# Routed experts behind gated linear attention: a tile's rows scaled on ScalarE, summed and written during the next tile

## The chip, the cores and the metric

The kernel runs on one core of a Trainium2 chip. The metric is device time in microseconds, the median of three runs. Before the change these were 812.84, 816.72 and 817.99 us, so the median is 816.72 us.

## The reference

Two blocks follow each other. The first is a gated linear recurrence per batch element and head; the second sends each row of its output to the two best of eight experts (noisy top-2 router) and adds the two weighted answers. All arrays are float32.

```
# attention: B, H, S, D = 4, 8, 768, 48
for t in range(S):
    state = alpha[:, :, t, :, None] * state + einsum('bhd,bhe->bhde', k[:, :, t], v[:, :, t])
    y[:, :, t] = einsum('bhd,bhde->bhe', q[:, :, t], state)
x = y.transpose(0, 2, 1, 3).reshape(3072, 384)

# router and experts: E = 8, F = 1024
noisy = x @ w_gate + log1p(exp(x @ w_noise)) * noise
top2 = the two largest of noisy per row;  w = softmax over these two
out[row] = sum over its two experts e of w_e * (relu(x[row] @ w1[e]) @ w2[e])
```

Each of the 3072 rows is answered by two experts, so every row of `out` is the sum of two weighted terms.

## The kernel before

**The recurrence** goes by 24 chunks of 128 time steps. `fast_gla` gives small functions (`load`, `load_v`, `alphas`, `keys`, `queries`, `scores`, `state`, `output`, ...) that the main loop at the end calls in a written-out order, several chunks deep. `load(n)` brings alpha, k and q of chunk n through the SP queue (L163), `load_v(n)` its v (L167). v of chunk 0 is first read by the matmuls of `state(0)` (L354).

**Routing.** After every three chunks the two experts of each row are found, and an entry (row, weight, expert, rank) is written to a table in DRAM that is sorted by expert (L138). `plan_tiles` then cuts the table into tiles of 128 entries of one expert. These tiles, not the rows in their first order, are the units of the expert work. With this data 51 tiles run.

**A tile i of the experts** is a chain over all engines. Its functions, with the engines they run on:

- `load_tab` (SP, L740): the 128 entries of the tile; `gather_x` (VectorE L757 to L763, then GpSimd L765): which rows these are, and an indirect DMA that gathers the rows of x; `load_w1` (SP, L748): the 1.5 MB of the expert's first matrix, in two buffers.
- `turn_x` (TensorE L774, VectorE L776): x transposed into `xt`, of which there is one buffer.
- `layer1` in two parts (TensorE L785, ScalarE L787): 48 matmuls of 128 columns, ReLU out of PSUM into `h`.
- `layer2` in two parts (TensorE L797): 16 matmuls of 384 columns into `o_ps`. The pool of `o_ps` has one buffer, so the first matmul of the next tile's `layer2` waits until `o_ps` has been read.
- `get_first` (GpSimd L804): an indirect DMA that reads, for entries that are their row's second answer, what the first answer left in `out`, into `prev` (two buffers). It waits for every earlier write to `out`, so for that of the tile before too.
- `combine` (GpSimd L814, VectorE L815, GpSimd L816): `prev` times 0 or 1 (no first answer, or one), then `o_ps` times the weight plus `prev`, then an indirect DMA that writes the rows to `out`.

`tile_steps` groups these into four steps per tile; engines work through their instructions in the order in which the code issues them. Tiles 0 to 9 are issued in between the last pieces of the recurrence and the routing (the main loop hands out the steps of two tiles per round from round 23 on), all later ones alone. The helper `few` borrows a buffer of `h_ps` for small router results (L620, L621, L665, read on VectorE by L622 and L667).

```
        def third():
            if i + 1 < units[1]:
                turn_x(i + 1)
            get_first(i)
            layer2(i, 0)

        def fourth():
            layer2(i, 1)
            combine(i)
```

So GpSimd's order in a steady tile is: gather for tile i + 2, read of the first answers, their scaling, write of the result.

Of the kernel before, what the change touches and what calls it, by code (L numbers as in the profile page):

```python
# [9 lines left out]
F32 = mybir.dt.float32  # L10
U32 = mybir.dt.uint32
I32 = mybir.dt.int32
AF = mybir.ActivationFunctionType
ALU = mybir.AluOpType
# [4 lines left out]
def kernel(  # L19
# [29 lines left out]
    nc = tc.nc  # L49
    B, H, S, D = q.shape  # L50
    N, DM = out.shape
    E, _, F = moe_w1.shape
    C = 128
# [8 lines left out]
    NU = NT // UC  # L62
# [6 lines left out]
    NTILE = (2 * N) // C + E - 1  # L69
    ALWAYS = (2 * N) // C + (E - 1) // 2  # L70
# [6 lines left out]
    def pool(name, bufs, on=ctx, **kw):  # L77
        return on.enter_context(tc.tile_pool(name=name, bufs=bufs, **kw))
# [557 lines left out]
    def put_some(n):  # L636
        for place, entry in to_put[:n]:
            put_entries(place, entry)
        del to_put[:n]
# [83 lines left out]
    def experts(on):  # L723
        one, two, three = on["one"], on["two"], on["three"]
        NB = 3
        x_in = [one.tile([C, DM], F32, name=f"x_in{i}") for i in range(NB)]
        prev = [one.tile([C, DM], F32, name=f"prev{i}") for i in range(2)]
# [1 line left out]
            nc.gpsimd.memset(t, 0.0)  # L729
        WHY = "computed from the counts, in range by construction"  # L730
        tabs, w1s, xts, os_, wheres = {}, {}, {}, {}, {}
        puts, gets = [], []

        def load_tab(i, units):
            if i >= NTILE:
# [67 lines left out]
        def get_first(i):  # L803
# [4 lines left out]
                tc.add_manual_dep(get.ins, put.name, AFTER, reason="reads rows of any earlier tile")  # L808
            gets.append(get.ins)

        def combine(i):
            o_ps, tab, where = os_.pop(i)["ps"], tabs.pop(i), wheres.pop(i)
            rows = prev[i % 2]
            nc.gpsimd.tensor_scalar(out=rows, in0=rows, scalar1=tab[:, 6:7], scalar2=None, op0=ALU.mult)  # L814
            nc.vector.scalar_tensor_tensor(rows, o_ps, tab[:, 1:2], rows, op0=ALU.mult, op1=ALU.add)  # L815
            put = nc.gpsimd.indirect_dma_start(out=out, out_offset=bass.IndirectOffsetOnAxis(ap=where[:, 0:1], axis=0),  # L816
                                               in_=rows, in_offset=None, bounds_check=N - 1, oob_is_err=False)
            for earlier in puts + gets:
                tc.declare_no_dep(put.ins, earlier, reason="different rows, or one that this tile has read")
            puts.append(put.ins)  # L820

        return load_tab, load_w1, gather_x, turn_x, layer1, layer2, get_first, combine


    def tile_steps(i, do, units):
        load_tab, load_w1, gather_x, turn_x, layer1, layer2, get_first, combine = do

        def first():
            if i + 1 < units[1]:
                load_w1(i + 1)  # L830
            if i + 2 < units[1]:
                gather_x(i + 2, units[0])
            layer1(i, 0)

        def second():
            layer1(i, 1)

        def third():
            if i + 1 < units[1]:
                turn_x(i + 1)  # L840
            get_first(i)
            layer2(i, 0)

        def fourth():
            layer2(i, 1)
            combine(i)

        return [first, second, third, fourth]

# [8 lines left out]
    def last_tiles(i, do):  # L858
        if i == NTILE:
            return  # L860
        number = nc.values_load(tiles_i[0:1, 0:1], min_val=0, max_val=NTILE,
                                skip_runtime_bounds_check_because="a count of tiles")
        with tc.If(number > i):
            do[0](i, NU)
            do[1](i)
            do[2](i, NU)
            do[3](i)
            for step in tile_steps(i, do, (NU, i + 1)):
                step()
            last_tiles(i + 1, do)  # L870


    def again_by_levels():
        with ExitStack() as es:
            on = pool("g_clear", 1, es)
            clear_table(on)
        with ExitStack() as es:
            general_gla(es)
        with ExitStack() as es:
            do = experts(pools(es, "g_"))  # L880
            for i in range(4):
                do[0](i, NU)
            do[1](0)
            for i in range(2):
                do[2](i, NU)
            do[3](0)
            for i in range(NTILE):
                do[0](i + 4, NU)
                for step in tile_steps(i, do, (NU, NTILE)):
                    step()  # L890


    with ExitStack() as es:
# [3 lines left out]
        do = experts(on)  # L897
        load_tab, load_w1, gather_x, turn_x = do[:4]
# [4 lines left out]
        def steps_of(i, n):  # L903
            units = NU if n >= NT + 4 else unit_of[i] + 1
            limit = min(ALWAYS, GIVEN[units - 1])
            steps = tile_steps(i, do, (units, limit))
            if i + 4 < limit:
                steps[0] = lambda go=steps[0]: (load_tab(i + 4, unit_of[i + 4] + 1), go())
            return steps
# [7 lines left out]

        with tc.manual_schedule():
            load(0)
            load(1)  # L920
            load_v(0)
            for n in range(2):
                alphas(n)
                keys(n)
# [6 lines left out]
            for n, tiles in enumerate(beside):  # L931
# [8 lines left out]
                last = [lambda: give(n - 3), lambda: put_some(UC)]  # L940
# [66 lines left out]
```

## Time and profile before

| what | value |
|---|---|
| median of three runs | 816.72 us (812.84 to 817.99) |
| the profiled execution | 817.13 us |
| its span, first to last instruction | 815.4 us |
| TensorE busy over the span | 758.8 us (93%) |
| GpSimd / VectorE / ScalarE busy | 347.4 us (43%) / 261.5 us (32%) / 168.8 us (21%) |
| mean granted TensorE clock, as a share of full speed | 0.974 |

The profiled execution is 0.4 us above the median and its span 1.7 us shorter than its own time; what lies outside the span belongs to start and end of the program. A share of busy time is a mean over stages: the first 210 us are recurrence and routing, from then to 800 us expert tiles follow each other. In the rows, PE is TensorE, PEld its weight loads, DVE VectorE, ACT ScalarE, POOL GpSimd, SP the queue that issues most DMAs. The time in square brackets is what the engine sat idle just before, and behind the arrow stands what ended that. A buffer that VectorE releases may be named by an instruction of VectorE just behind the one that did it.

### The profile page before, as it was taken

The page shows a single profiled execution, that of the slowest core. Times are in us where ns is not written, and L with a number is a line of the kernel's source. Part 1 is how long each engine was busy: PE and PEld are TensorE (multiplying, and loading weights), DVE is VectorE, ACT ScalarE, POOL GpSimd, SP SyncE. Part 2 cuts the span into 40 slices and gives each one's busy share as a digit, 9 for nine tenths or more (in the row PEclk, how much of TensorE's full clock was granted, in tenths as well). Part 3 has the DMA queues.
Part 4 walks back from the last instruction along what each step waited for, and adds up shares of the span by engine and source line. Part 5 has one row for each costly group of instructions (what it writes and reads, how often), then busy time and mean ns, then how long its engine had stood idle before and what let it go on. Part 6 is the DMA issues. An engine that isn't in the chain of part 4 may idle for free. (4 is left out here: it accounts for less than half of the span.)

```text
span 815.4 us, 14294 instructions
## 1 busy us (share of the span) xinstructions
PE 758.8 (93%) x5239; PEld 622.7 (76%) x5239; DVE 261.5 (32%) x858; ACT 168.8 (21%) x332; POOL 347.4 (43%) x439
## 2 busy tenths in 40 slices
PE   5999999998999898999999999999999999999992
PEld 4888888887888586877787867787777778777781
DVE  6778877898310224101111011110111111111100
ACT  2465535644111110100111001110011110101100
POOL 4326754656342544434343334433343433433331
PEclk9999979999899999999999999999999999999997
DMA  9999888986645444455445654455554455555420
GB/s 154 173 214 178 201 186 180 186 178 189 229 121 181 150 164 148 159 186 201 165 166 193 210 187 153 167 184 196 182 193 154 157 191 205 208 196 204 161 95 12
DMA packets 152160, 141.76 MB, mean 174 GB/s; under 512 B 114861, under 2 KB 126735, under 8 KB 152084
## 3 DMA queue, kind: packets, MB, share of 16 engines
q1 hardware_dynamic: 139744, 116.51, 51.1%
q0 software_dynamic: 11328, 23.72, 8.1%
q8 instruction: 45, 0.74, 0.4%
q10 hardware_dynamic: 1012, 0.53, 0.3%
q14 instruction: 31, 0.25, 0.1%
HBM read 131.95 MB, written 15.25 MB: 181 GB/s over the span
## 5 line engine op out<-in xcount | busy, mean ns | idle before, releaser
L785 PEld LDWEIGHTS h_ps<-xt,w 128*128 128x128 f32 x2448 | 282.9, 193 | 18.2 <-DVE picked L622 3.9
L797 PE MATMUL o_ps<-w,h 128*128 x816 | 275.3, 491 | 16.7 <-DVE tab L759 16.2
L785 PE MATMUL h_ps<-xt,w 128*128 128x128 f32 x2448 | 284.4, 276 | 5.0 <-DVE picked L622 3.8
L797 PEld LDWEIGHTS o_ps<-w,h 128*128 128x128 f32 x816 | 151.6, 191 | 115.8 <-ACT h L787 11.1
L815 DVE SCALAR_TENSOR_TENSOR prev<-o_ps,tab,prev 128x384 f32<-128x384 f32 x51 | 31.5, 618 | 466.8 <-POOL prev L814 427.5
L787 ACT ACTIVATE h<-h_ps 128x512 f32<-128x512 f32 x102 | 60.9, 598 | 510.7 <-PE h_ps L785 510.7
L814 POOL TENSOR_SCALAR prev<-prev,tab 128x384 f32<-128x384 f32 x51 | 63.5, 1246 | 141.8 <-DMA prev<-out_dram,where 141.8
L804 POOL DMA_INDIRECT prev<-out_dram,where x51 | 51.2, 1004 | 133.2 <-DMA out_dram<-prev,where 131.8
L816 POOL DMA_INDIRECT out_dram<-prev,where x51 | 55.6, 1091 | 56.7 <-DVE tab L759 43.6
L765 POOL DMA_INDIRECT x_in<-x_rows,where x51 | 53.2, 1043 | 25.7 <-issue 12.3
L138 POOL DMA_INDIRECT table<-entry,place_u x48 | 54.1, 1127 | 15.5 <-issue 11.2
L305 POOL TENSOR_TENSOR k_P<-k_P,over 128x512 f32<-128x512 f32 x24 | 28.6, 1191 | 40.5 <-DVE over L292 39.3
L776 DVE COPY xt<-x_ps 128x384 f32<-128x384 f32 x51 | 28.2, 552 | 28.0 <-PE x_ps L774 27.6
L286 DVE TENSOR_TENSOR_SCAN P_all<-a_all,least 128x516 f32<-128x516 f32 x24 | 31.0, 1294 | 10.6 <-ACT a_all L283 9.5
L328 PE MATMUL sc<-q_P,k_P 48*128 48x128 f32 x384 | 31.6, 304 | 1.7 <-DVE MT L333 1.6
L333 DVE COPY_PREDICATED MT<-upto,sc 128x512 f32<-128x512 uint32 x48 | 32.2, 725 | 0.6 <-PE sc L328 0.6
L292 DVE TENSOR_TENSOR_SCAN over<-a_all,P_all 128x515 f32<-128x515 f32 x24 | 31.7, 1322 | 0.8
L359 POOL TENSOR_TENSOR S<-S,end 128x384 f32<-128x384 f32 x20 | 20.3, 1015 | 26.3 <-DVE S L357 26.2
L328 PEld LDWEIGHTS sc<-q_P,k_P 48*128 48x128 f32 x384 | 26.3, 204 | 6.7 <-issue 5.7
L214 PE MATMUL y<-MT,vt 128*48 128x128 f32 x384 | 27.7, 290 | 0.0
L210 PE MATMUL y<-q_P,S 128*128 128x128 f32 x192 | 27.5, 289 | 0.0
L354 PE MATMUL o_ps<-vt,k_end 128*128 128x96 f32 x160 | 23.1, 291 | 3.6 <-ACT k_end L342 3.6
(145 smaller groups left out, 599.4 us busy)
## 6 DMA issues: line engine op xcount, KB each, us to landing
w<-in_moe_w_dram SPq DMA_DIRECT2D x51, 1536.0 KB, 7.5
w<-in_moe_w_dram SPq DMA_DIRECT2D x32, 384.0 KB, 5.7
a_in<-in_alpha_dram SPq DMA_DIRECT2D x24, 192.0 KB, 5.2
k_in<-in_k_dram SPq DMA_DIRECT2D x24, 192.0 KB, 5.2
q_in<-in_q_dram SPq DMA_DIRECT2D x24, 192.0 KB, 5.3
vt<-in_v_dram SPq DMA_DIRECT2D x24, 192.0 KB, 4.7
x_rows<-y_sb SPq DMA_DIRECT2D x24, 192.0 KB, 3.1
tab<-table SPq DMA_DIRECT2D x51, 2.0 KB, 1.6
```

Source lines behind the costliest of these rows:

```text
L138: put = nc.gpsimd.indirect_dma_start(out=table, out_offset=bass.IndirectOffsetOnAxis(ap=place, axis=0), in_=entry, in_offset=None, bounds_ ...
L292: nc.vector.tensor_tensor_scan(over.rearrange("p j t -> p (j t)")[:, :0:-1], a_all[:, :1:-1], P_all[:, :1:-1], 0.0, op0=ALU.mult, op1=ALU.max)
L328: nc.tensor.matmul(c["sc"][i][:, j, :], c["k"][r, j, :], c["q"][r, j, :], start=True, stop=True)
L333: nc.vector.copy_predicated(MTs[n % 2][:, i], mask_upto, sc)
L765: nc.gpsimd.indirect_dma_start(out=x_in[i % NB], out_offset=None, in_=x_rows[0:units * UT, :], in_offset=bass.IndirectOffsetOnAxis(ap=wher ...
L785: nc.tensor.matmul(h_ps[:, fo, :], w1[:, a, ds((part * FO // 2 + fo) * C, C)], xt[:, a, :], start=a == 0, stop=a == KO - 1)
L787: nc.scalar.activation(os_[i]["h"][part], h_ps, AF.Relu)
L797: nc.tensor.matmul(o["ps"], o["h"][part][:, f, :], w2[:, ds(o["e"], 1), fo, :].rearrange("p o d -> p (o d)"), start=fo == 0, stop=fo == FO ...
L804: get = nc.gpsimd.indirect_dma_start(out=prev[i % 2].bitcast(U32), out_offset=None, in_=out.bitcast(U32), in_offset=bass.IndirectOffsetOnA ...
L814: nc.gpsimd.tensor_scalar(out=rows, in0=rows, scalar1=tab[:, 6:7], scalar2=None, op0=ALU.mult)
L815: nc.vector.scalar_tensor_tensor(rows, o_ps, tab[:, 1:2], rows, op0=ALU.mult, op1=ALU.add)
L816: put = nc.gpsimd.indirect_dma_start(out=out, out_offset=bass.IndirectOffsetOnAxis(ap=where[:, 0:1], axis=0), in_=rows, in_offset=None, bo ...
```

## The change

`combine` is cut in two. A new function `scale` reads `o_ps` on ScalarE right after the tile's second layer, multiplies it by the weight and leaves the result `o` in SBUF (two buffers, shared with `y_sb`). `combine` then adds on VectorE alone (`prev` times 0 or 1, plus `o`) and writes; it is issued in the second step of the next tile. `get_first` moves from the third step to behind `scale`. The last tiles (`last=True`: 49 and 50, and the branches that do not run here) keep the order of before, with the scaling of `prev` on VectorE in place of GpSimd. And `load_v(0)` is issued ahead of `load(1)`.

```
+        def scale(i):
+            os_[i]["o"] = two.tile([C, DM], F32, tag="y_sb", name="o")
+            nc.scalar.activation(os_[i]["o"], os_[i]["ps"], AF.Copy, scale=tabs[i][:, 1:2])
+
         def combine(i):
-            o_ps, tab, where = os_.pop(i)["ps"], tabs.pop(i), wheres.pop(i)
-            rows = prev[i % 2]
-            nc.gpsimd.tensor_scalar(out=rows, in0=rows, scalar1=tab[:, 6:7], scalar2=None, op0=ALU.mult)
-            nc.vector.scalar_tensor_tensor(rows, o_ps, tab[:, 1:2], rows, op0=ALU.mult, op1=ALU.add)
+            o, tab, where, rows = os_.pop(i), tabs.pop(i), wheres.pop(i), prev[i % 2]
+            if "o" in o:
+                nc.vector.scalar_tensor_tensor(rows, rows, tab[:, 6:7], o["o"], op0=ALU.mult, op1=ALU.add)
+            else:
+                nc.vector.tensor_scalar(out=rows, in0=rows, scalar1=tab[:, 6:7], scalar2=None, op0=ALU.mult)
+                nc.vector.scalar_tensor_tensor(rows, o["ps"], tab[:, 1:2], rows, op0=ALU.mult, op1=ALU.add)
...
         def second():
             layer1(i, 1)
+            if i - 1 in waiting:
+                waiting.remove(i - 1)
+                combine(i - 1)
 
         def third():
             if i + 1 < units[1]:
                 turn_x(i + 1)
-            get_first(i)
+            if last:
+                get_first(i)
             layer2(i, 0)
 
         def fourth():
             layer2(i, 1)
-            combine(i)
+            if last:
+                combine(i)
+            else:
+                scale(i)
+                get_first(i)
+                waiting.append(i)
...
-            steps = tile_steps(i, do, (units, limit))
+            steps = tile_steps(i, do, (units, limit), i >= ALWAYS - 2)
...
             load(0)
+            load_v(0)
             load(1)
-            load_v(0)
```

On GpSimd, in the steady tiles, the order before is this (L765 gathers x for a later tile, L804 reads the first answers, L814 scales them, L816 writes the result; `prev_188` and `prev_189` are the two buffers of `prev`):

```order
L765 DMA x_in_186<-x_rows,where 128x384
L804 DMA prev_189<-out_dram,where 128x384
L814 TENSOR_SCALAR prev_189<-prev_189,tab 128x384
L816 DMA out_dram<-prev_189,where 3072x384
L765 DMA x_in_187<-x_rows,where 128x384
L804 DMA prev_188<-out_dram,where 128x384
```

After the change it is this (L822 is the write):

```order
L765 DMA x_in_186<-x_rows,where 128x384
L822 DMA out_dram<-prev_189,where 3072x384
L804 DMA prev_188<-out_dram,where 128x384
L765 DMA x_in_187<-x_rows,where 128x384
L822 DMA out_dram<-prev_188,where 3072x384
```

The scaling has left GpSimd, the write of a tile stands behind the gather that was behind it before, and the read of the next tile's first answers follows the write with nothing between.

On VectorE the sum of a tile stood before the change behind the copy of the next tile's `xt`, and ahead of the gather's five instructions and the next `xt`:

```order
L776 COPY xt<-x_ps 128x384
L815 SCALAR_TENSOR_TENSOR prev_188<-o_ps,tab,prev_188 128x384
L757 SCALAR_TENSOR_TENSOR other,tab<-expert_idv,tab,given 128x8
L759 MEMSET tab 128x1
L760 TENSOR_TENSOR tab<-tab 128x1
L761 TENSOR_TENSOR tab<-tab 128x1
L763 SCALAR_TENSOR_TENSOR where<-tab 128x2
L776 COPY xt<-x_ps 128x384
```

After the change the sum (L818) stands behind the gather's instructions and just ahead of the next `xt`, and it reads `o` in place of `o_ps`:

```order
L776 COPY xt<-x_ps 128x384
L757 SCALAR_TENSOR_TENSOR other,tab<-expert_idv,tab,given 128x8
L759 MEMSET tab 128x1
L760 TENSOR_TENSOR tab<-tab 128x1
L761 TENSOR_TENSOR tab<-tab 128x1
L763 SCALAR_TENSOR_TENSOR where<-tab 128x2
L818 SCALAR_TENSOR_TENSOR prev_188<-prev_188,tab,o 128x384
L776 COPY xt<-x_ps 128x384
```

The gather no longer waits on VectorE for the sum of the tile before; the copy of `xt` still does.

On ScalarE each tile gains one instruction, behind the two ReLUs (L787) of its first layer. At tiles 1 to 3, between which the recurrence still sends its last copies, the order is now:

```order
L813 ACTIVATE o<-o_ps,tab 128x384
L787 ACTIVATE h_2901<-h_ps 128x512
L233 COPY lgs_113<-h_ps 128x16
L787 ACTIVATE h_2902<-h_ps 128x512
L217 COPY yT<-y 128x512
L226 COPY y_sb<-tp 128x384
L813 ACTIVATE o<-o_ps,tab 128x384
```

What moved: the only reader of `o_ps` is now L813 on ScalarE, behind no DMA's landing of its own tile. TensorE's order is the same as before.

## Rows read from the trace of the kernel before

**Rows 1.** Window of expert tiles: TensorE, loads, VectorE, ScalarE, GpSimd busy us, clock, DMA.
```profile
304.95:801.00 496.05, 478.24 (x2902) 380.78 (x2900) 77.96 (x365) 51.93 (x87) 195.99 (x185) 1.00 0.50 176
```

**Rows 2.** Waits of TensorE, 225 to 801 us: total us, times, longest.
```profile
PE o_ps L797 <- DVE tab L759: 16.2, 17, 1.8
PE h_ps L785 <- DVE picked L622: 3.8, 1, 3.8
PE h_ps L785 <- DVE again L397: 0.5, 1, 0.5
PE o_ps L797 <- DVE prev L815: 0.4, 1, 0.4
```

**Rows 3.** Timeline of TensorE: start us, us; layer 2 of four tiles, layer 1 of one.
```profile
322.07 5.33 PE L797 MATMUL o_ps<-w,h 128*128 x16
327.23 5.52 PE L785 MATMUL h_ps<-xt,w 128*128 128x128 f32 x48
332.92 5.33 PE L797 MATMUL o_ps<-w,h 128*128 x16
...
784.13 5.33 PE L797 MATMUL o_ps<-w,h 128*128 x16
```

**Rows 4.** Costliest groups of the page, GpSimd's of a tile: busy, mean ns, idle before.
```profile
L814 POOL TENSOR_SCALAR prev<-prev,tab 128x384 f32<-128x384 f32 x51 | 63.5, 1246 | 141.8 <-DMA prev<-out_dram,where 141.8
L804 POOL DMA_INDIRECT prev<-out_dram,where x51 | 51.2, 1004 | 133.2 <-DMA out_dram<-prev,where 131.8
L816 POOL DMA_INDIRECT out_dram<-prev,where x51 | 55.6, 1091 | 56.7 <-DVE tab L759 43.6
L765 POOL DMA_INDIRECT x_in<-x_rows,where x51 | 53.2, 1043 | 25.7 <-issue 12.3
```

**Rows 5.** Timeline of GpSimd, one round from a write to the next.
```profile
356.90 1.09 POOL L816 DMA_INDIRECT out_dram<-prev,where  x1 [0.93 <-DVE tab L759]
...
362.43 1.00 POOL L804 DMA_INDIRECT prev<-out_dram,where  x1 [3.09 <-DMA out_dram<-prev,where]
...
366.66 1.25 POOL L814 TENSOR_SCALAR prev<-prev,tab 128x384 f32<-128x384 f32 x1 [3.22 <-DMA prev<-out_dram,where]
...
368.84 1.09 POOL L816 DMA_INDIRECT out_dram<-prev,where  x1 [0.93 <-DVE tab L759]
```

**Rows 6.** Source lines L804 (first row) and L816 (second): landing of 51 DMAs each.
```profile
DMA to landing us min/median/max: 2.1/3.1/6.9
```
```profile
DMA to landing us min/median/max: 2.7/5.2/8.2
```

**Rows 7.** Timeline of TensorE, two stalls among the first tiles.
```profile
280.46 7.09 PE L797 MATMUL o_ps<-w,h 128*128 x16 [1.71 <-DVE tab L759]
...
314.65 7.25 PE L785 MATMUL h_ps<-xt,w 128*128 128x128 f32 x48 [3.80 <-DVE picked L622]
```

**Rows 8.** Groups by line, 195 to 260 us: ScalarE's copy of 128x384 out of PSUM.
```profile
L226 ACT COPY y_sb<-tp 128x384 f32<-128x384 f32 x4 | 1.9, 479 | 6.7 <-PE tp L224 6.7
```

**Rows 9.** Timeline, VectorE's two-operand instructions beside GpSimd's, two places.
```profile
196.12 2.65 DVE L760 TENSOR_TENSOR tab<-tab 128x1 f32<-128x1 f32 x1
...
197.54 1.20 POOL L305 TENSOR_TENSOR k_P<-k_P,over 128x512 f32<-128x512 f32 x1
...
222.40 1.10 POOL L816 DMA_INDIRECT out_dram<-prev,where  x1 [2.52 <-DVE tab L759]
...
222.58 0.15 DVE L593 TENSOR_TENSOR den<-entry 128x3 f32<-128x3 f32 x1
```

**Rows 10.** Timeline of the start: issue of v, chunk 1's alpha, first use of v.
```profile
5.89 1.15 SPq L167 DMA_DIRECT2D vt<-in_v_dram  x1
...
7.74 1.09 PE L275 MATMUL tp<-ident,a_in 128*128 128x128 f32 x4
...
18.38 2.02 PE L354 MATMUL o_ps<-vt,k_end 128*128 128x96 f32 x8 [3.64 <-ACT k_end L342]
```

**Rows 11.** Timeline of the end: the last tile's sum.
```profile
800.08 0.62 DVE L815 SCALAR_TENSOR_TENSOR prev<-o_ps,tab,prev 128x384 f32<-128x384 f32 x1 [8.24 <-PEq L969]
```

More of the change, by code (lines that the diff above doesn't have):

```diff
@@ L731, in experts @@
         tabs, w1s, xts, os_, wheres = {}, {}, {}, {}, {}
-        puts, gets = [], []
+        puts, gets, waiting = [], [], []
         def load_tab(i, units):
@@ L820, in combine, with tile_steps @@
             puts.append(put.ins)
-        return load_tab, load_w1, gather_x, turn_x, layer1, layer2, get_first, combine
-    def tile_steps(i, do, units):
-        load_tab, load_w1, gather_x, turn_x, layer1, layer2, get_first, combine = do
+        return load_tab, load_w1, gather_x, turn_x, layer1, layer2, get_first, scale, combine, waiting
+    def tile_steps(i, do, units, last=False):
+        load_tab, load_w1, gather_x, turn_x, layer1, layer2, get_first, scale, combine, waiting = do
         def first():
@@ L867, in last_tiles @@
             do[3](i)
-            for step in tile_steps(i, do, (NU, i + 1)):
+            for step in tile_steps(i, do, (NU, i + 1), True):
                 step()
@@ L888, in again_by_levels @@
                 do[0](i + 4, NU)
-                for step in tile_steps(i, do, (NU, NTILE)):
+                for step in tile_steps(i, do, (NU, NTILE), i >= NTILE - 1):
                     step()
```

## Prediction

> **What bounds the kernel now.** I read the table by stretch first, then TensorE's waits, then the timeline of one tile, then GpSimd's groups. From 305 us on TensorE is busy 478.2 of 496.1 us at full clock [rows 1]: the expert tiles are nearly bound by TensorE. An undisturbed tile takes 332.92 - 322.07 = 10.85 us from one second layer to the next [rows 3]. But from 322.07 to 784.13 us 41 tiles pass (counted on the timeline), which is 462.06 / 41 = 11.27 us each, 0.42 us more than the floor.
>
> The waits tell who adds it: 17 times the first matmul of a second layer waits for `o_ps`, 16.2 us together, never over 1.8 us [rows 2]. `o_ps` is freed by the sum on VectorE, which waits for GpSimd's scaling of `prev`, which waits for the read of the first answers to land (141.8 us of idle time over 51 tiles), and that read waits for the tile before to be written (131.8 us, 45 times) [rows 4]. This is a ring that closes on itself through DRAM. One round of it, from write to write [rows 5]: 5.53 us until the read may issue, 4.23 until it has landed, 1.25 scaling, 0.93 for the sum and its hand-over, in all 368.84 - 356.90 = 11.94 us. By the means of the groups [rows 4]: write 1.09, gap and gather 0.3 + 1.04, idle 131.8 / 45 = 2.93, so 5.36 to the read; read 1.00 and idle 141.8 / 51 = 2.78, so 3.78 to its landing; scaling 1.25; sum 0.93: 11.32 us. That agrees with the 11.27 us per tile. So the ring, not TensorE, sets the pace now, by a small margin.
>
> **The change, part by part.**
>
> *The ring without the scaling.* GpSimd's 1.25 us leave it: 11.32 - 1.25 = 10.07 us, below TensorE's 10.85. More important, `o_ps` no longer hangs on the ring. It is freed by ScalarE some 0.5 us after the second layer's end: the trace has no such scaling, but its nearest row is a copy of the same shape out of PSUM at 0.48 us [rows 8], and nothing of the tile's DMAs stands ahead of it. The next second layer begins 332.92 - 327.23 = 5.69 us after this point [rows 3], so 5 us of cover are left. ScalarE is busy 52 of 496 us [rows 1]; 49 scalings add some 24 us to it, all beside matmuls.
>
> *What becomes late next.* The sum still stands ahead of the next copy of `xt` on VectorE, so a ring that lags would reach TensorE there. The copy is due when the next first layer starts, 10.85 us after the second layer's end; the sum can begin 0.5 us after that end. This leaves some 9 us of slack, where the sum before had 5.69 us until the next second layer, and a ring of 10.07 us gains 0.8 us on TensorE in each tile. Behind the waiting sum are the `xt` copy and the table arithmetic; behind GpSimd's read, which waits for the write, is the gather for three tiles on, which has over two tiles of time. I take no stall from either in the steady stretch.
>
> *The gain in the steady stretch.* 462.06 - 41 x 10.85 = 17.2 us. Of this 17.8 - 3.8 - 1.0 = 13.0 us are idle time (the window's idle, less the stall at 314.65, less its end behind the last matmul) [rows 1, 2], the rest is TensorE filling up again behind each wait.
>
> *The gain among the first tiles.* The wait of 3.8 us at 314.65 is for VectorE to read a router result out of a buffer of `h_ps`; it stood behind the sum of a tile, hence behind the ring. The first layer behind it took 7.25 us where 5.52 is usual, so 1.7 us more went to a lower clock [rows 3, 7]. After the change that sum is the one of the tile before, done long ago: 5.5 us gained. Four more waits before 305 us, 20.9 - 13.0 - 3.8 = 4.1 us by the rows of waits, go in the same way, with 1.8 us of low clock (7.09 against 5.33 [rows 3, 7]) and some 0.3 us of refill each (4.2 us for about 15 waits above): 7.1 us.
>
> The two slow pieces each start behind a stall, of 1.71 and 3.80 us [rows 7]; what each lost, 1.7 us, is what some 3.5 us at 1.2 in place of 2.4 GHz lose. In the stretch where TensorE is busiest the granted clock is 1.00 [rows 1]. The Trainium skill, TensorE: Matmul & The Clock Gate, Part 1, says that the gate follows how busy the array was, and that how many matmuls run at the low clock differs from run to run. By the row both low stretches go with their stalls; by that rule they may come elsewhere, and the time would be 3.5 us more than my sum.
>
> *What stays or comes new.* A small wait at the router results, as VectorE must still read them: an estimate of 0.5 us at two places from the 0.5 us wait of the third of these rows [rows 2]. The one long piece of table arithmetic on VectorE can delay a sum and so an `xt` copy: between 0 and the 3.8 us of the wait it replaces; I take 1 us, since 9 us of slack stand against it. Together 2.
>
> *v of chunk 0 earlier.* Its first reader starts at 18.38 us and waited for ScalarE's `k_end`, not for v, which was issued at 5.89 [rows 10]: nothing to gain. Alpha, k and q of chunk 1 are issued later by v's 1.15 us, and alpha's transposes at 7.74 can slip by as much. The chain to `k_end` goes through other waits on the way, so this costs between 0 and 1.2 us; I take 0.
>
> *The end.* The last two tiles keep the old order; the last sum started at 800.08, 0.1 us behind the last matmul, and VectorE had sat idle for 8.24 us before it [rows 11]. With the scaling of `prev` on VectorE instead of GpSimd this stays: 0, between -0.5 and +1.
>
> *Sum.* 817.13 - 17.2 - 5.5 - 7.1 + 2 = 789.3 us for the profiled execution. It stood 0.4 us above the median: 789.
>
> **The rivals.**
>
> *Only the steady stretch gains (14%).* The first tiles share VectorE and GpSimd with table writes and planning, and the sum still stands in VectorE's order between them. If their stalls stay, 12.6 us are not gained: 801. For it: a read can take up to 6.9 us to land [rows 6]. Against it: 9 us of slack.
>
> *A port shared by VectorE and GpSimd lengthens the ring (3%).* The new sum reads two operands from SBUF. At 196.12 us a two-operand instruction of one column took 2.65 us, until GpSimd's arithmetic at 197.54 was over; at 222.58 one took 0.15 us beside an indirect write issued at 222.40 [rows 9]. So arithmetic blocks it, the issue of an indirect DMA does not. If it did, 1.04 us more in the ring make 11.1, a pace 0.25 over the floor on 47 tiles, 12 us: 801. The Trainium skill, SBUF — State Buffer, "Who interferes with whom", says that a VectorE instruction with two SBUF inputs contends with a GpSimd instruction that reads SBUF. The first pair of rows agrees with it, the second does not show it for an indirect DMA.
>
> *Slower: the read is caught behind the load of w1 (4%).* The sum would come right after the second layer, the write 1 us later, and the read at about the time when the next 1.5 MB load starts. Landings of reads range from 2.1 to 6.9 us and of writes from 2.7 to 8.2 [rows 6], so such a load can delay them. The ring of 10.07 us becomes slower than today's 11.27 once landings cost 1.2 us more in the mean; at 2.2 us more it is 12.3, 1.0 us over today's pace on 48 tiles: about 865, less some 12 for the early stalls, 850. Against it: the write would leave that load's time as the read enters it, and the sum of both is what counts; today the write has the longer landing (median 5.2 against 3.1).
>
> *Nothing is gained (5%).* The wait moves from `o_ps` to `xt` with the same length: 808 to 825. For it: VectorE's order still has the sum ahead of `xt`. Against it: the slack above.
>
> **How the numbers follow.** The main case has 74%: 789, with 784 to 797 for its own unknowns (no stall left and the refill fully gained, against the low clock elsewhere, 1.2 at the start and a few small stalls). The two cases at 801 hold 17%. A range from 783 to 802 holds all three but their tails. About 1% (8 us) is what a measurement can tell from no change: faster by more has 74 + 14 + 3 = 91%, within 1% the 5% of no gain, slower 4%.
>
> **What would show it.** Right: no waits of a second layer for VectorE; second layers 10.85 us apart through the steady stretch; TensorE idle there below 3 us of some 480; sums on VectorE about 1 us behind ScalarE's scaling or up to a few us later, with `xt` never waited for; writes 10.85 us apart on average. Wrong: TensorE waiting for `xt` (L776), or writes over 11 us apart with reads landing late, or waits for `o_ps` that now end with ScalarE.

## The result, and the profile after

| | before | after |
|---|---|---|
| median, same chip | 817.36 us (812.84 to 820.64) | 787.92 us (787.72 to 788.86) |
| profiled execution | 817.13 us | 788.10 us |
| TensorE busy over the span | 758.8 us (93%) | 750.6 us (95%) |
| GpSimd / VectorE / ScalarE busy | 347.4 / 261.5 / 168.8 us | 280.0 / 264.9 / 197.0 us |

The ratio after to before is 0.9646, with a 95% interval from 0.9598 to 0.9693: faster by 3.5%. The forecast was 789 us. Six of the nine runs of E12, the last experiment below, (831 to 834 us) count as slow, being over 1.5% above its fastest, and stand outside its ratio; every other run is fast.

TensorE's waits come first. The whole execution after the change has eight rows of them; these two are those of the expert tiles (what was waited for; total us, times, longest):

```profile
PE x_ps L774 <- DMA x_in<-x_rows,where: 0.7, 1, 0.7
PE h_ps L785 <- DVE xt L776: 0.7, 1, 0.7
```

All waits of the eight rows lie before 212 us, in the recurrence, the routing and the first tile. Every row of [rows 2] is gone, and nothing has taken its place. The windows say the same (length; busy us of TensorE, its loads, VectorE, ScalarE, GpSimd; clock, DMA share, GB/s):

```profile
225.00:300.00 75.00, 75.00 (x487) 61.26 (x488) 15.26 (x82) 16.84 (x30) 26.67 (x30) 1.00 0.54 169
300.00:400.00 100.00, 99.91 (x614) 79.98 (x614) 22.50 (x108) 15.97 (x27) 34.85 (x36) 1.00 0.55 190
400.00:500.00 100.00, 100.00 (x611) 79.88 (x611) 15.15 (x72) 15.98 (x27) 27.70 (x28) 1.00 0.55 199
500.00:600.00 100.00, 100.00 (x626) 80.90 (x625) 15.76 (x73) 16.56 (x28) 28.06 (x28) 1.00 0.50 177
```

TensorE idles 0.09 us in these 375 us and not at all from 600 to 771 us, where it idled 17.8 of 496 [rows 1]. The second layers that answer to [rows 3] start here:

```profile
310.30 5.33 PE L797 MATMUL o_ps<-w,h 128*128 x16
...
755.20 5.33 PE L797 MATMUL o_ps<-w,h 128*128 x16
```

That is (755.20 - 310.30) / 41 = 10.85 us per tile, the pace of an undisturbed tile. TensorE is the bound from the first tile to the last.

At the router result, where the stall of 3.80 us stood [rows 7], the first layer now follows the read of the result at once (timeline, the same place in the program):

```profile
304.25 0.20 DVE L622 TENSOR_TENSOR picked<-picked,h_ps 128x48 f32<-128x48 f32 x1 [4.96 <-PE h_ps L621]
304.51 5.43 PEld L785 LDWEIGHTS h_ps<-xt,w 128*128 128x128 f32 x48 [0.18 <-DVE picked L622]
304.51 5.62 PE L785 MATMUL h_ps<-xt,w 128*128 128x128 f32 x48
```

The groups of a tile, which answer to [rows 4] (busy, mean ns, idle before):

```profile
L818 DVE SCALAR_TENSOR_TENSOR prev<-prev,tab,o 128x384 f32<-128x384 f32 x49 | 30.3, 619 | 263.7 <-DMA prev<-out_dram,where 150.9
L822 POOL DMA_INDIRECT out_dram<-prev,where x51 | 52.3, 1025 | 185.1 <-DVE prev L818 164.9
...
L804 POOL DMA_INDIRECT prev<-out_dram,where x51 | 52.4, 1027 | 124.1 <-DMA out_dram<-prev,where 115.7
L813 ACT ACTIVATE o<-o_ps,tab 128x384 f32<-128x384 f32 x49 | 28.5, 581 | 225.0 <-PE o_ps L797 210.6
```

The ring through DRAM is still there: sums wait for reads (150.9 us), reads for writes (115.7 us). It no longer reaches TensorE. One round, which answers to [rows 5] (SPq is SP issuing DMAs; L748 is the load of a tile's 1,536 KB of w1, and L740, further below, that of its table):

```profile
404.05 0.62 DVE L818 SCALAR_TENSOR_TENSOR prev<-prev,tab,o 128x384 f32<-128x384 f32 x1 [5.52 <-DMA prev<-out_dram,where]
...
404.95 1.02 POOL L822 DMA_INDIRECT out_dram<-prev,where  x1 [4.66 <-DVE prev L818]
...
407.82 1.02 POOL L804 DMA_INDIRECT prev<-out_dram,where  x1 [1.85 <-DMA out_dram<-prev,where]
407.94 0.38 SPq L748 DMA_DIRECT2D w<-in_moe_w_dram  x1
...
415.67 0.62 DVE L818 SCALAR_TENSOR_TENSOR prev<-prev,tab,o 128x384 f32<-128x384 f32 x1 [6.30 <-DMA prev<-out_dram,where]
```

From write to read it now takes 2.87 us, where [rows 5] have 5.53; from read to sum 7.85, where they have 4.23 and the scaling. The round of two transfers has changed its phase to the load of w1, as the DMA view of 400 to 420 us shows (40 slices of 0.5 us; busy share in tenths, GB/s):

```profile
DMA  9999999100010910016689999999600000107307
GB/s 426 410 410 426 433 408 372 34 0 0 16 4 0 350 43 0 0 25 57 172 352 426 418 426 393 454 383 415 260 26 27 6 0 0 4 0 276 117 0 66
```

The write of 404.95 has the engines to itself (the lone slice at 350 GB/s). The read of 407.82 goes out beside the load of 407.94, and its sum starts after the load's stretch has ended. Before the change the write was the one that met the load.

The end stands as it was (the row that answers to [rows 11]; the last matmul ends at 771.05 us):

```profile
771.08 0.62 DVE L821 SCALAR_TENSOR_TENSOR prev<-o_ps,tab,prev 128x384 f32<-128x384 f32 x1 [3.53 <-PE o_ps L797]
```

Where the 29.0 us of the profiled executions came from, between starts of second layers:

| stretch | before | after | gained |
|---|---|---|---|
| start to the first expert tile | 216.06 | 216.97 | -0.9 |
| first expert tile to the first steady one | 106.0 | 93.3 | 12.7 |
| 41 steady tiles | 462.1 | 444.9 | 17.2 |
| the rest to the end | 33.0 | 32.9 | 0.1 |

### The profile page after: what moved, and what is told of

The parts are those of the page before. It is cut to its first block, busy times and chain, and to the rows that moved or that the text cites. A ratio compares the mean times of both kernels' runs of the same rounds, so it can differ in the third digit from the quotient of the medians.

```text
span 786.4 us, 14341 instructions
## 1 busy us (share of the span) xinstructions
PE 750.6 (95%) x5239; PEld 619.7 (79%) x5239; DVE 264.9 (34%) x860; ACT 197.0 (25%) x381; POOL 280.0 (36%) x388
## 4 chain that ended last, share of the span: by engine, by line
PE 83%; DVE 8%; DMA 3%; issue 1%; POOL 1%; ACT 1%; ACTq 0%; SPq 0%; DVEq 0%; POOLq 0%
PE h_ps L785 35%; PE o_ps L797 33%; PE tp L275 3%; PE x_ps L774 2%; DVE over L292 2%; PE o_ps L354 2%; DVE P_all L286 2%; PE sc L328 2%; PE y L214 2%; PE y L210 1%; PE h_ps L232 1%; DVE MT L333 1%; DMA table<-entry,place_u 1%; DMA x_in<-x_rows,where 1%; PE tp L224 1%
## 5 line engine op out<-in xcount | busy, mean ns | idle before, releaser
L797 PE MATMUL o_ps<-w,h 128*128 x816 | 272.0, 486 | 0.0
L797 PEld LDWEIGHTS o_ps<-w,h 128*128 128x128 f32 x816 | 150.9, 190 | 94.1 <-ACT h L787 0.2
L818 DVE SCALAR_TENSOR_TENSOR prev<-prev,tab,o 128x384 f32<-128x384 f32 x49 | 30.3, 619 | 263.7 <-DMA prev<-out_dram,where 150.9
L822 POOL DMA_INDIRECT out_dram<-prev,where x51 | 52.3, 1025 | 185.1 <-DVE prev L818 164.9
L787 ACT ACTIVATE h<-h_ps 128x512 f32<-128x512 f32 x102 | 60.9, 597 | 227.8 <-PE h_ps L785 204.5
L804 POOL DMA_INDIRECT prev<-out_dram,where x51 | 52.4, 1027 | 124.1 <-DMA out_dram<-prev,where 115.7
L813 ACT ACTIVATE o<-o_ps,tab 128x384 f32<-128x384 f32 x49 | 28.5, 581 | 225.0 <-PE o_ps L797 210.6
L765 POOL DMA_INDIRECT x_in<-x_rows,where x51 | 51.6, 1011 | 67.5 <-DVE where L763 49.6
L138 POOL DMA_INDIRECT table<-entry,place_u x48 | 53.9, 1124 | 16.4 <-issue 11.4
L286 DVE TENSOR_TENSOR_SCAN P_all<-a_all,least 128x516 f32<-128x516 f32 x24 | 31.0, 1292 | 11.2 <-ACT a_all L283 7.0
L292 DVE TENSOR_TENSOR_SCAN over<-a_all,P_all 128x515 f32<-128x515 f32 x24 | 34.2, 1426 | 0.8
L359 POOL TENSOR_TENSOR S<-S,end 128x384 f32<-128x384 f32 x20 | 20.3, 1013 | 27.2 <-DVE S L357 27.1
L774 PE MATMUL x_ps<-ident,x_in 128*128 128x128 f32 x153 | 25.1, 273 | 0.7 <-DMA x_in<-x_rows,where 0.7
```

Source lines behind the costliest of these rows:

```text
L138: put = nc.gpsimd.indirect_dma_start(out=table, out_offset=bass.IndirectOffsetOnAxis(ap=place, axis=0), in_=entry, in_offset=None, bounds_ ...
L286: nc.vector.tensor_tensor_scan(P_all[:, 0:NP * CB], a_all[:, 0:NP * CB], least.rearrange("p j t -> p (j t)"), 0.0, op0=ALU.mult, op1=ALU.max)
L292: nc.vector.tensor_tensor_scan(over.rearrange("p j t -> p (j t)")[:, :0:-1], a_all[:, :1:-1], P_all[:, :1:-1], 0.0, op0=ALU.mult, op1=ALU.max)
L765: nc.gpsimd.indirect_dma_start(out=x_in[i % NB], out_offset=None, in_=x_rows[0:units * UT, :], in_offset=bass.IndirectOffsetOnAxis(ap=wher ...
L774: nc.tensor.transpose(x_ps[:, a, :], x_in[i % NB][:, ds(a * C, C)], ident)
L787: nc.scalar.activation(os_[i]["h"][part], h_ps, AF.Relu)
```

## The experiments

Ratios are against the kernel before on the same chip, with their 95% intervals; its medians were 823.09 us beside E1 to E4, 821.7 beside E5 to E8 and 820.34 beside E9 to E12. E7 and E8 have two runs each, all others three or more. Theory: the ring through DRAM set the pace, and the change wins because the ring got shorter and `o_ps` no longer hangs on it.

**E1 and E2: v of chunk 0, alone and left out.** E1 is the kernel before with

```
             load(0)
+            load_v(0)
             load(1)
-            load_v(0)
```

and E2 is the changed kernel with these lines as they were before.

> The kernel before, with only the load of v of chunk 0 moved ahead of chunk 1. Theory (v gains nothing, its first reader waits for k_end): 816 to 818 us, the first state matmul (L354) still at about 18.4 us, alpha's transposes of chunk 1 about 1.1 us later than 7.74. Rival (v is part of the gain): 2 us or more off, and L354 earlier than 18.4.

> The changed kernel, with v of chunk 0 loaded behind chunk 1 again. Theory: 787 to 788.5 us, the same as the changed kernel within 1 us, and no wait of TensorE for a second layer. Rival (the new order of loads costs or gains at the start): 1 us or more off in the first second layer's start (216.97 us now).

E1: 821.45 us, ratio 0.999 (0.9956 to 1.0023). E2: 790.03 us, 0.9603 (0.9576 to 0.963). So the move of v does nothing that can be measured; all of the gain is in the tiles. In E1 the first reader of v started at 18.42 us, against 18.38 [rows 10], and waited for ScalarE's `k_end` as before; the transposes of chunk 1's alpha started at 8.84 us in place of 7.74, the 1.1 us later that were expected.

E2 also has the landings that answer to [rows 6], here from 350 to 700 us, first of its reads (L804), then of its writes (L822):

```profile
DMA to landing us min/median/max: 2.1/4.3/7.1
```

```profile
DMA to landing us min/median/max: 2.4/2.6/6.0
```

The median write lands in half the time, the median read takes longer.

**E3: only the ring is shortened.** In the kernel before, the scaling of `prev` goes from GpSimd (1.25 us) to VectorE (0.42 us), so the ring is 0.83 us shorter; `o_ps` is still freed by the sum, in its old place.

```
-            nc.gpsimd.tensor_scalar(out=rows, in0=rows, scalar1=tab[:, 6:7], scalar2=None, op0=ALU.mult)
+            nc.vector.tensor_scalar(out=rows, in0=rows, scalar1=tab[:, 6:7], scalar2=None, op0=ALU.mult)
```

> The kernel before, with only the scaling of prev moved from GpSimd to VectorE (0.42 us in place of 1.25): the ring is 0.83 us shorter, o_ps still hangs on it. Theory (the ring sets the pace, and o_ps passes every late landing on): 0.83 us off each of the 15 steady waits, of which up to 1.76 us remain, so about 3 us of waits in place of 13, and half of the early stalls: 797 to 803 us. Rival (only the early release of o_ps counts): 812 us or more.

797.75 us, 0.9691 (0.9657 to 0.9726). The first two of four rows of TensorE's waits after 225 us:

```profile
PE h_ps L785 <- DVE picked L622: 2.3, 1, 2.3
PE o_ps L797 <- DVE tab L759: 1.6, 2, 1.1
```

16.2 us of waits for `o_ps` [rows 2] have become 1.6. Moving this one instruction was worth 25 us; the rest of the change adds about 8 more (790 in E2). Two things are in these 25 us that E3 does not tell apart: the ring is 0.83 us shorter, and its write has mostly left the load of w1. From 350 to 700 us the median read is issued 2.9 us behind its write, where it was 5.5 us before.

**E4: the changed kernel with read and sum in their old place.** ScalarE's `scale` stays; `get_first` goes back to the third step, `combine` to the fourth.

```
 def third():
-    if last:
-        get_first(i)
+    get_first(i)
 def fourth():
-    if last:
-        combine(i)
-    else:
+    if not last:
         scale(i)
-        get_first(i)
-        waiting.append(i)
+    combine(i)
```

> The changed kernel, but the read of first answers and the sum are issued where they were before (third and fourth step of the same tile), not beside the next tile; o_ps is still scaled by ScalarE and GpSimd scales nothing. Theory (the release of o_ps and the shorter ring do it, the place of the sum does not): 787 to 790 us, no waits for o_ps. Rival (the sum must stand beside the next tile to be hidden): 795 us or more, with waits for the copy of xt or for o_ps.

790.67 us, 0.9609 (0.9587 to 0.9632), the same as E2. With the short ring the sum needs no other place.

**E5: only `o_ps` is freed early.** E4, but with the old GpSimd scaling kept and a plain addition behind it, so the ring has its old length.

```
-                nc.vector.scalar_tensor_tensor(rows, rows, tab[:, 6:7], o["o"], op0=ALU.mult, op1=ALU.add)
+                nc.gpsimd.tensor_scalar(out=rows, in0=rows, scalar1=tab[:, 6:7], scalar2=None, op0=ALU.mult)
+                nc.vector.tensor_tensor(rows, rows, o["o"], op=ALU.add)
```

> The kernel before, with only o_ps scaled by ScalarE at once (VectorE then adds two tiles of SBUF); GpSimd's scaling of prev, the read and the sum stay in their old places. The ring keeps its 11.32 us. Theory (a ring over 10.85 us lags 0.47 us per tile, 9 us of slack take the first 19 tiles, then the copy of xt passes it on): early stalls gone, 10 us of the steady loss left: about 797 us (794 to 802), with waits of TensorE for xt late in the run. Rival 1 (only o_ps counts): 788. Rival 2 (only the ring's length counts): 814 or more.

850.66 us, 1.0309 (1.0228 to 1.039): slower than before, which nothing had foreseen. TensorE waits for no `o_ps`; it waits for `x_in`, whose gather is queued on GpSimd among the ring's instructions:

```profile
PE x_ps L774 <- DMA x_in<-x_rows,where: 30.9, 25, 3.6
```

The ring itself had become slower than before: from 350 to 700 us it takes 12.2 us in the mean from write to write, where it took 11.2. The timeline shows where:

```profile
508.46 0.33 SPq L740 DMA_DIRECT2D tab<-table  x1
508.46 0.56 DVE L819 TENSOR_TENSOR prev<-prev,o 128x384 f32<-128x384 f32 x1 [12.31 <-POOL prev L818]
...
509.30 1.10 POOL L823 DMA_INDIRECT out_dram<-prev,where  x1 [0.87 <-DVE tab L759]
509.35 0.38 SPq L748 DMA_DIRECT2D w<-in_moe_w_dram  x1
...
516.72 1.00 POOL L804 DMA_INDIRECT prev<-out_dram,where  x1 [4.98 <-DMA out_dram<-prev,where]
```

The load of w1 is issued 0.05 us behind the write, and the read has to wait 7.4 us. In the kernel before (timeline, at the round of [rows 5]) there is more between them:

```profile
356.00 0.62 DVE L815 SCALAR_TENSOR_TENSOR prev<-o_ps,tab,prev 128x384 f32<-128x384 f32 x1 [11.48 <-POOL prev L814]
356.65 0.33 SPq L740 DMA_DIRECT2D tab<-table  x1
...
357.54 0.38 SPq L748 DMA_DIRECT2D w<-in_moe_w_dram  x1
```

There the load comes 0.64 us behind the write of 356.90, and the read 5.53 us behind it. The landings of the write, 350 to 700 us, before and in E5 (us, min/median/max):

```profile
DMA to landing us min/median/max: 3.7/5.2/6.7
```

```profile
DMA to landing us min/median/max: 6.1/6.8/8.4
```

What sets the load's start is a buffer. SP issues its DMAs in order, and w1's load stands behind that of a small table, which waits for one of six table buffers to be released by its last reader. Before, that reader is the sum; in E5 the addition doesn't read the table, so it is GpSimd's scaling, one step earlier. The first row of SP's waits from 350 to 700 us, before and in E5:

```profile
SPq L740 <- DVE tab L760: 303.1, 31, 12.4
```

```profile
SPq L740 <- POOL prev L818: 247.8, 29, 10.9
```

(L760, named in the first row, belongs to the table arithmetic that follows the sum on VectorE. The sum above ends at 356.62 us, 0.03 us before the table's load goes out.) This left two readings of E5: the load's new start, or the old place of the sum. E9 and E10 are made to tell them apart.

**E6 and E7: the changed kernel with a longer ring.** One GpSimd scaling ahead of the sum, then two.

```
+                nc.gpsimd.tensor_scalar(out=rows, in0=rows, scalar1=tab[:, 6:7], scalar2=None, op0=ALU.mult)
                 nc.vector.scalar_tensor_tensor(rows, rows, tab[:, 6:7], o["o"], op0=ALU.mult, op1=ALU.add)
```

> The changed kernel, with one scaling of prev put back on GpSimd between the read's landing and the sum (1.25 us more in the ring, and nothing else moved). Theory: ring of about 11.3 us, as above: 793 to 800 us, no waits for o_ps, a few for xt late in the run. Rival (with o_ps free the ring is hidden for good): 788 to 789.

> The changed kernel with two such scalings on GpSimd (2.5 us more in the ring; the second multiplies by the same 0 or 1 again). Theory: ring of about 12.5 us, 1.7 us per tile over the floor on 48 tiles, less 9 us of slack: about 860 us (835 to 870), TensorE waiting for xt from about the sixth tile on. Rival (slack renewed each tile): 788 to 792.

E6: 798.58 us, 0.9704 (0.962 to 0.9789). E7: 864.91 us, 1.0504 (1.0396 to 1.0612). E7's first row of TensorE's waits:

```profile
PE h_ps L785 <- DVE xt L776: 53.7, 37, 4.7
```

From 350 to 700 us E6's ring takes 11.0 us in the mean from write to write, 0.15 over TensorE's pace. The slack in front of `xt` takes up part of that: TensorE waits for `xt` only four times, 5.5 us in all, and E6 is at 798.6 us where E2 is at 790.0. A ring of 12.3 us (E7) it cannot take up: every tile falls further behind, and the wait comes where the forecast said it would come next.

**E8: the kernel before without the loads of w1.** From the third tile on a tile takes the buffer of the tile two earlier, and with it a wrong matrix, so that only the time means anything.

```
+            if i - 2 in w1s:
+                w1s[i] = w1s[i - 2]
+                return
             w1s[i] = two.tile([C, KO, F], F32, name="w1")
```

> The kernel before, but the first matrix is loaded only for the first two tiles and used again for all later ones, so the 1.5 MB loads, and the right answer of later tiles, are left out. Theory (half of the ring is waiting behind these loads): write to read 3.0 us in place of 5.4, the ring 8 to 9.5 us, no steady waits for o_ps, 788 to 795 us. Rival (the landings are as long without them): ring near 11.3, 810 us or more.

790.29 us, 0.9598 (0.9509 to 0.9687), with the ring of before, GpSimd's scaling in it. One write and its read (L819, L807 there):

```profile
502.56 1.10 POOL L819 DMA_INDIRECT out_dram<-prev,where  x1 [4.44 <-DVE tab L762]
...
505.50 1.00 POOL L807 DMA_INDIRECT prev<-out_dram,where  x1 [0.50 <-DMA out_dram<-prev,where]
```

2.94 us from write to read, against 5.4 by the means of before. So the load costs the ring some 2.5 us a tile, twice what the scaling costs; without either, TensorE is the bound. From 350 us on the round is TensorE's 10.85 us; the 8 to 9.5 us expected of the ring itself show only in two rounds that catch up, of 8.1 us each.

**E9 and E10: place of the sum against start of the load.** E9 is E5 (old place, old length) with a sum that reads the table again; E10 is E6 (new place, old length) with the plain addition that doesn't.

```
 E9, from E5
-                nc.vector.tensor_tensor(rows, rows, o["o"], op=ALU.add)
+                nc.vector.scalar_tensor_tensor(rows, rows, tab[:, 6:7], o["o"], op0=ALU.mult, op1=ALU.add)
 E10, from E6: these two lines the other way round
```

> As the run with o_ps freed alone (851 us: o_ps to ScalarE, everything else in its old place, GpSimd scaling prev), but the sum on VectorE reads the tile's table again (it multiplies by the same 0 or 1 once more), so the table's buffer comes free at the sum's end and not at the end of GpSimd's scaling, 0.6 us later. SP's next table load waits for that buffer, and the 1.5 MB load of w1 stands behind it on SP. Theory A (the load then starts 0.6 us behind the write in place of beside it, and the write lands in 5.5 us in place of 7.0): 795 to 812 us. Theory B (the old place of sum and write delays the gather of x): 840 us or more, with TensorE waiting for x as before.

> As the changed kernel with one scaling put back on GpSimd (798.6 us), but the sum on VectorE no longer reads the table, so the buffer comes free at the end of GpSimd's scaling, before the write is issued. Theory A: the w1 load starts beside the write, write to read 7 us in place of 5.5, ring of 12 us or more: 835 to 860 us, TensorE waiting for xt. Theory B (the place alone makes the difference): 795 to 803 us.

E9: 806.11 us, 0.9847 (0.9766 to 0.9928). E10: 860.72 us, 1.0487 (1.0424 to 1.055), just over the 860 of its theory A. With the old length of ring and `o_ps` freed by ScalarE:

| | table released by the sum | released ahead of the sum |
|---|---|---|
| sum in the old place | E9: 806 us | E5: 851 us |
| sum in the new place | E6: 799 us | E10: 861 us |

The column decides, not the row. E10's timeline has the load 0.04 us behind the write, and the read 7.56 us behind it:

```profile
510.44 1.09 POOL L823 DMA_INDIRECT out_dram<-prev,where  x1 [0.87 <-DVE prev L819]
510.48 0.38 SPq L748 DMA_DIRECT2D w<-in_moe_w_dram  x1
...
518.00 1.04 POOL L804 DMA_INDIRECT prev<-out_dram,where  x1 [6.47 <-DMA out_dram<-prev,where]
```

E6, where the sum still reads the table, has it 0.63 us behind, and the read 5.57 us:

```profile
506.88 1.10 POOL L823 DMA_INDIRECT out_dram<-prev,where  x1 [0.93 <-DVE prev L819]
507.51 0.38 SPq L748 DMA_DIRECT2D w<-in_moe_w_dram  x1
...
512.45 1.05 POOL L804 DMA_INDIRECT prev<-out_dram,where  x1 [4.47 <-DMA out_dram<-prev,where]
```

**E11 and E12: seven table buffers in place of six**, E11 in E5 and E12 in the kernel before.

```
-"tab": pool(name + "tab", 6, es)
+"tab": pool(name + "tab", 7, es)
```

> As the run with o_ps freed alone (851 us), with 7 buffers for the table and the row numbers in place of 6: SP's table load no longer waits for the sum of two tiles ago. Theory A: w1 loads start at the end of the first layer whatever the sum does, write to read back to 3 to 5.5 us: 790 to 806 us, SP waiting for TensorE before its w1 loads. Theory B: 840 us or more.

> The kernel before with 7 such buffers in place of 6, nothing else. Theory A (the w1 load tied to the sum is what makes write to read 5.4 us and the ring 11.3): write to read nearer 3 us in the steady stretch, 796 to 808 us. Rival (the collision comes anyway, since the sum falls near the end of the first layer): 813 us or more.

E11: 796.33 us, 0.9712 (0.9652 to 0.9772): the same E5 kernel is 54 us faster once the load doesn't hang on the table. The load then waits for the buffer of w1 itself, released by TensorE's first layer (SP, 350 to 700 us; L774 are the transposes behind that layer):

```profile
SPq L748 <- PE x_ps L774: 286.7, 32, 9.4
```

The load now goes out ahead of the write, by 0.8 to 5.4 us. The read follows the load's issue by 7.1 to 9.0 us, 7.4 in the median; so the write still waits beside the load, but less long than in E5: the median read is issued 6.0 us behind its write, where E5 has 7.1.

E12: ratio 1.0006 (0.9918 to 1.0095; nine runs from 814.57 to 834.26 us), where the theory had 796 to 808 us, so the theory missed. Its load also waits for TensorE (277.5 us, 29 times), but the waits for `o_ps` stay:

```profile
PE o_ps L797 <- DVE tab L759: 18.3, 17, 2.5
```

Its timeline has two phases. From 360 to 492 us TensorE waits for nothing, with GpSimd's scaling in the ring and `o_ps` freed by the sum as before. From the write of 368.88 us on the load stands 3.5 to 4.4 us behind the write, and from 378.87 to 465.64 us all eight rounds take 10.85 us:

```profile
454.80 1.09 POOL L816 DMA_INDIRECT out_dram<-prev,where  x1 [2.47 <-DVE tab L759]
...
457.76 1.00 POOL L804 DMA_INDIRECT prev<-out_dram,where  x1 [0.53 <-DMA out_dram<-prev,where]
...
459.18 0.38 SPq L748 DMA_DIRECT2D w<-in_moe_w_dram  x1
```

Behind the write of 465.64 us GpSimd issues the gather 2.2 us later than usual (what held it, the profile does not show). The read goes out at 470.62 us, 0.6 us behind a load, and its sum comes 8.7 us later. From then on write and load mostly lie within 2 us of each other, and the waits return:

```profile
503.15 0.38 SPq L748 DMA_DIRECT2D w<-in_moe_w_dram  x1
...
503.52 1.09 POOL L816 DMA_INDIRECT out_dram<-prev,where  x1 [0.93 <-DVE tab L759]
...
511.36 1.00 POOL L804 DMA_INDIRECT prev<-out_dram,where  x1 [5.40 <-DMA out_dram<-prev,where]
```

So even the long ring of the kernel before keeps TensorE's pace while the write does not meet the load, as in E8. The seventh buffer unties the load from the table, but it does not choose the phase. Why the second phase holds is argued and not shown: there the write follows the sum, and so does TensorE, for which the load waits, so write and load stay close. No run tried that apart.

## Why the prediction was right

**The ring sets the pace (11.32 us by its parts): right.** Moving GpSimd's 1.25 us alone (E3) or taking out the load's disturbance alone (E8) brings the tiles to TensorE's pace or close to it; putting the scaling back into the changed kernel makes the ring 11.0 us (E6), twice 12.3 (E7). How long the shortened ring is by itself can be read from the changed kernel: from 346.68 to 501.25 us all but one of 15 sums wait for the read and not for ScalarE, and a round takes 10.30 us in the mean. The forecast had 10.07.

**`o_ps` freed by ScalarE 0.5 us after the second layer: right in kind.** The scaling takes 0.58 us where the copy in [rows 8] took 0.48; 0.1 us more, all of it beside matmuls. (The Trainium skill, ScalarE: Activation LUTs, What ACT_TABLE_LOAD costs, says that each scale or bias read from a pointer adds about 93 ns; the trace agrees, 581 against 479 ns.) On its own, with the load where it was (E9), this part is worth only 1.5% (0.7 to 2.3% by its interval): a ring slower than TensorE is then hidden by the slack for a while and reaches TensorE elsewhere. Taken singly, the short ring was the larger part (E3, 3.1%), its new place beside the loads included.

**`xt` is late next, with some 9 us of slack: right.** The changed kernel does not wait there after its first tile; E7 and E10, with rings over 12 us, wait exactly there (53.7 us in E7). With the sum in its old place the slow ring comes through the gather of x instead, for which TensorE waits 30.9 us in E5 and 6.5 us in E9.

**The steady stretch: 17.2 us forecast, 17.2 measured.**

**The first tiles: 12.6 us less 2 for what stays or comes new, so 10.6; 12.7 measured.** The mis-sized term is the 2 us. There is no wait at a router result after 225 us and no late `xt`: since the sum ahead of the router's instructions is now one that could start long before, all that is left is 0.18 us of a weight load, where [rows 7] has 3.80. The 2 us were not far off for every execution: E2's, the same but for v, has 1.9 us of waits after 225 us, for x and `xt`. The two low-clock stretches of [rows 7] went with their stalls; all windows from 225 us on have a granted clock of 1.00. The case that they come elsewhere did not occur here. The 2.1 us more gained here and the 0.9 us lost at the start partly cancel in the total.

**v: 0 forecast.** E1 and E2 agree with it within their intervals. The profiled execution reached the first second layer 0.9 us later, E1 0.8 us later and E2, without the move, 0.0 us; but E4, which has the move, was there 0.3 us earlier, and E3, which doesn't have it, 3.2 us later. It stays open whether the move costs the bounded 0 to 1.2 us.

**The rival "read caught behind the load of w1" was half right.** The read is caught: 7.85 us from its issue to the sum in the round above. But the write is free in exchange (2.87 us), and the sum of both, with the 0.90 us hand-over, is what counts, as the forecast held against this rival. In the round above that sum is 11.62 us, more than a tile; the next takes 10.08, and the mean of 10.30 is what keeps the ring ahead of TensorE. From 511 us on the sum waits for ScalarE's scaling, and the round stays at TensorE's pace but for one of 11.31 us: writes at 523.43, 534.28 and 545.12 us. SP's load then waits for TensorE too, and goes out 3.84 us behind the write in all rounds but one. The other mechanism that could make it slower was not among the rivals: a change of the table's last reader. In the changed kernel the sum still reads the table, so that it did not happen; in E5 and E10 it did, and cost 45 and 62 us.

**The shared port: did not happen.** The sum with two operands from SBUF takes 0.62 us as the one before did [rows 11]. Three of its 49 executions stand beside GpSimd's issue of an indirect DMA and take no longer (617 to 619 ns); none stands beside GpSimd's arithmetic, so that case was not tried. The forecast read its row at 196.12 us too firmly: GpSimd's arithmetic (L359) began only at 196.75, and until then GpSimd was issuing an indirect DMA (L138).

The step of the forecast that was right for an incomplete reason is the ring's composition. It took 5.36 and 3.78 us as prices of a write and a read. They are prices of a phase: the transfer that meets the load pays. E12 shows it within one run.

The four kernels near 790 us (E2, E4, E8 and the changed kernel itself) have TensorE as the bound; by their intervals none of them is faster than another, and no other version that was run comes as low.

## What to carry to other kernels

Where tiles pass a result through DRAM to the next tile, add up the whole round from row means and compare it with the pace of the busiest engine; an instruction in a round that is longer can cost its length in every tile, down to that pace, whatever its engine's busy share. Before changing which instruction reads a small buffer last, look at what its release lets go: on an in-order queue the big load behind the small one can start with it. When a term is the landing of a DMA, look at which large transfer lies beside it, since a shift of 0.6 us can move the cost from one transfer to another, or add it.

## What was not expected of the hardware

- When the read that follows a write through DRAM can be issued hangs on a large load (1,536 KB) beside it. From 350 to 700 us the median is 2.9 to 3.0 us behind the write's issue without such loads (E8) or with one 1.5 us or more behind the write (after the change), 5.5 us with one 0.6 us behind it (before, E6, E9; 3.1 to 7.0 in single rounds), and 7.1 us with one issued with it (E5, E10; 7.4 and 7.6 in the rows above). E5's write lands when the load is through, as its DMA view of 500 to 520 us shows (slices of 0.5 us; both were issued between 509.3 and 510.4, the read at 516.72):

```profile
DMA  9999710000065100000179569999999930000001
GB/s 377 418 429 422 295 60 32 24 0 0 0 129 227 37 0 0 0 0 1 3 66 82 164 254 352 377 377 434 408 427 399 389 127 15 0 0 1 0 0 33
```

- The Trainium skill, DMA: Bandwidth & Descriptors, Queues, rings and completion order, says that a DMA engine takes turns between the queues it has work for, packet by packet. Taken alone, this would let one expect that a small write is held up by a part of a large load. E5's median landing is 6.8 us against the 2.6 of E2, 4.2 us more, and 1,536 KB take some 3.7 us at the 420 GB/s of the fullest slices (an estimate from the row above): about all of the load. No run here shows the packets of the two queues one by one, so why is open.
- 0.6 us in the start of a load, set by which instruction releases a 2 KB table, moved the time by 45 and 62 us (E5 against E9, E10 against E6).
